# Moving the copies of ten units' transposed q and k from VectorE to ScalarE, with twelve buffers instead of eight for the loads of q and k

## The chip, the core and the metric

The kernel runs on one core of a Trainium2 chip. The engines have short names here: PE is TensorE's matmul and PEld its weight load, DVE is VectorE, ACT is ScalarE, POOL is GpSimd, SP is SyncE. Each engine works through its own list of instructions in order and waits on semaphores for the others. The metric is the device time in microseconds of one execution; the median of three is 149.7 us (148.23 to 149.87).

## The reference

Two stages are chained. The first is attention inside chunks of 64 positions, for 8 batches, 8 heads and 9 chunks each, with a head dimension of 64:

```python
scores = scale * np.matmul(q_c, k_c.transpose(0, 1, 2, 4, 3))     # per chunk, 64 x 64
scores = scores - np.max(scores, axis=-1, keepdims=True)
attn = np.exp(scores)
attn = attn / (np.sum(attn, axis=-1, keepdims=True) + 1e-09)
out = np.matmul(attn, v_c)
```

Its output, put to x of shape (8, 576, 512), goes through a token mixer, batch by batch:

```python
wq = x @ w_q                                   # 512 -> 64
wk = x @ w_k
W_tok = scale * np.einsum('bsd,btd->bst', wq, wk)
mixed = np.einsum('bst,btd->bsd', W_tok, x)
return (np.maximum(mixed, 0.0) @ w_out).astype(np.float32)
```

## The kernel before

The attention is cut into 36 **units** of 16 chunks; four and a half units make a batch. A unit goes through a pipeline of stages, one unit entering in each **period** kk of the main loop:

- `stage_a1` (tile `tp`, L396): 16 transposes of the unit's q and k on PE, eight for q and then eight for k, into one of four PSUM banks of the pool that most other matmuls share.
- `stage_a2` (tile `qkt`, L406): one copy of 128x1024 f16 from that bank into SBUF, on DVE. This is the instruction that the change touches.
- `stage_b1`, `stage_b2`: the scores on PE (`sp`, L422), their maximum (`mx`, L430) and the subtraction (`sh`, L436) on DVE, the exponential on ACT (`es`, L444).
- `stage_c`: transposes of the exponentials on PE (`ep`, L452) and their copy on ACT (`et`, L454).
- `stage_d1`, `stage_d2`: the product with v on PE (`xp`, L468), with a column of ones that gives the denominator, and on DVE the sum, the reciprocal (L480, L482) and the scaling into `x_nat` (L483).

The program is recorded in the order in which it is written, so each engine's list has this order. In period kk that is: scores and maximum of unit kk, product with v of unit kk-2, the mixer's steps of place 0, transposes of unit kk+2, transposes and copy of the exponentials of unit kk-1, subtraction and exponential of unit kk, scaling of unit kk-2, the `qkt` copy of unit kk+2, and the mixer's steps of place 2. The start differs: period 0 also makes stage a of unit 1, and period 1 that of units 2 and 3. So the copy of unit u stands in period u-2 from unit 4 on.

The mixer of a batch begins when its units are done. `make_moe` holds its steps: transposes of x (`tx`, copy `xt` on ACT, L166), products with w_q and w_k (`wpa`, `wpb`, copies `wqkT`), transposes of wk (`wknp`, `wkn`), the product g (L271), the mixed rows (`ma`, relu `rmx`, L172) and the last product with w_out (`op`, L340, copy `osb`, store on SP's queue). `plan` gives each step a period. For batch 0 the first copy of x comes in period 4, the products with w_q and w_k in period 8, `rmx` in periods 11 and 12. After the last period the steps that are left are called in an order written by hand.

Loads of q, k and v change f32 to f16 and go through POOL's queue. Their order is a list sorted by the period of need, and `AHEAD` sets both how many buffers q and k have and how early a load is recorded:

```python
wanted = [(max(u - 2, 0), 1, load_qk, (u,)) for u in range(NU)]
...
        wanted.append((first + 2, 0, load_v, (b, part)))
wanted += [(8, 2, load_wqk, ()), (13, 2, load_wout, ())]
wanted.sort(key=lambda x: x[:2])
```

POOL's list holds hardly anything but these loads, so the recorded place of a load among the stages does not matter to it; what holds a load back is its waits. There are two kinds. A load into a buffer of q or k that was used before waits for the transposes (L396) of the unit that had it. And a load waits for the landing of the load eight places before it, since the loads share eight completion semaphores in turn. v has three buffers for each part. All loads of q and k after unit 0's are at L96, those of v at L106.

Of the kernel before, what the change touches and what calls it, by code (L numbers as in the profile page):

```python
# [17 lines left out]
def kernel(  # L18
# [16 lines left out]
    nc = tc.nc  # L35
# [9 lines left out]
    NU = B * NI // 8  # L45
    W0 = 5 * CH
    R, G = 4, 16
    AHEAD = 8
    scale_attn = 1.0 / math.sqrt(D)
    scale_moe = 1.0 / math.sqrt(DH)  # L50
    ds = bass.ds
# [1 line left out]
    const = ctx.enter_context(tc.tile_pool(name="const", bufs=1))  # L53
    qn_pool = ctx.enter_context(tc.tile_pool(name="qn", bufs=AHEAD))
    v_pool = ctx.enter_context(tc.tile_pool(name="vpool", bufs=3))
# [76 lines left out]
    def loads(before):  # L132
        while wanted and wanted[0][0] < before:
            _, _, load, args = wanted.pop(0)
            load(*args)
# [10 lines left out]
    make_identity(nc, ident[:])  # L146
    loads(AHEAD - 2)

# [16 lines left out]
    def copy(on_vector, to, of):  # L165
        (nc.vector.tensor_copy if on_vector else nc.scalar.copy)(to, of)  # L166
# [222 lines left out]
    def stage_a1(u):  # L389

        tp = bank([P, 2, 8, R, G], F16, name="tp")
        for ti in range(2):
            src = data[u, ti]
            for r in range(R):
                for sl in range(2):
                    nc.tensor.transpose(  # L396
                        tp[CH * sl : CH * sl + CH, ti, :, r, :],
                        src[:, sl, r * D : r * D + D],
                        ident[:],
                    )  # L400
        state[u] = {"tp": tp}

    def stage_a2(u):
        tp = state[u]["tp"]
        qkt = qkt_pool.tile([P, 2, 8, R * G], F16, name="qkt", tag="qkt")
        nc.vector.tensor_copy(  # L406
            qkt[:].rearrange("p t c k -> p (t c k)"),
            tp[:].rearrange("p t c r g -> p (t c r g)"),
        )
        state[u]["qkt"] = qkt  # L410
# [112 lines left out]
    def stage_a(u):  # L523
        stage_a1(u)
        loads(u - 1 + AHEAD)
        stage_a2(u)
# [4 lines left out]
    for kk in range(NU - 1):  # L531
        stage_b1(kk)
        if kk >= 2:
            stage_d1(kk - 2)
        fill(kk, 0, 0.0)
        if 2 <= kk < NU - 2:
            stage_a1(kk + 2)
            loads(kk + 1 + AHEAD)
        if kk >= 1:
            stage_c(kk - 1)  # L540
        stage_b2(kk)
        if kk >= 2:
            stage_d2(kk - 2)
        if 2 <= kk < NU - 2:
            stage_a2(kk + 2)
        for u in ((1,), (2, 3))[kk] if kk < 2 else ():
            stage_a(u)
        fill(kk, 2, 1.4 if len(outs) < 4 else 1.9)
# [17 lines left out]
    u = NU - 1  # L566
# [62 lines left out]
```

## Time and profile before

| | |
|---|---|
| median of 3 runs | 149.7 us (148.23 to 149.87) |
| profiled execution | 149.79 us, its span 148.0 us |
| busy PE / DVE / ACT / POOL | 123.6 / 114.4 / 101.7 / 86.4 us of the span |
| `qkt` copies on DVE (L406) | 36, 24.5 us, mean 680 ns |
| `et` copies on ACT (L454) | 36, 21.5 us, mean 597 ns; ACT idle before them 20.9 us |
| loads of q and k issued by POOL (L96) | 78, 56.1 us busy |

The span is what the trace covers; 1.79 us of the profiled time lie outside it. The page cuts the span into 40 slices of 3.7 us. A row of a group gives the line, engine, operation, tiles and shapes, the count, the busy time, the mean of one, and the idle time of the engine just before it with what ended that. A row of the timeline gives start, duration and the same idle time in brackets. Matmuls overlap, so the gap from one start to the next is what a matmul costs its engine, not its own duration. The same holds more weakly for DVE and ACT, where a duration reaches a little past the start of the next instruction.

### The profile page before, as it was taken

What the parts mean: (1) busy time and instruction counts of PE and PEld (TensorE: products, weight loads), DVE (VectorE), ACT (ScalarE), POOL (GpSimd) and SP (SyncE); (2) the same over time, 40 slices, a digit from 0 to 9 for tenths busy, and PEclk for the clock granted to TensorE, in tenths of its full rate; (3) what the DMA queues carried; (4) which work ended last, traced back from release to release, by engine and by line L of the source; (5) the groups of instructions that cost most, each with busy time, mean ns of one, the idle gap of its engine ahead of it and who ended that gap; (6) DMA issues with size and microseconds to landing.
All of it is one profiled execution on the core that took longest, in us unless ns stands there. A gap on an engine that the chain in (4) does not pass through costs nothing.

```text
span 148.0 us, 5933 instructions
## 1 busy us (share of the span) xinstructions
PE 123.6 (84%) x2516; PEld 82.6 (56%) x2516; DVE 114.4 (77%) x236; ACT 101.7 (69%) x200; POOL 86.4 (58%) x138
## 2 busy tenths in 40 slices
PE   0666999697779899899999999999949998999940
PEld 0454678475666556766576567655635464543420
DVE  0489899999999889989998999899876886156430
ACT  3140356378698699888988998799829995775320
POOL 6999999399996879499269857986000000000000
PEclk9999999779999999999999999999999999999999
DMA  4999999999999999999999999999990623234492
GB/s 141 137 159 161 165 178 166 117 118 149 154 157 185 187 205 228 212 213 207 200 238 187 196 247 220 157 240 200 212 148 21 192 95 126 79 138 142 173 296 104
DMA packets 64619, 25.35 MB, mean 171 GB/s; under 512 B 40528, under 2 KB 60112, under 8 KB 64592
## 3 DMA queue, kind: packets, MB, share of 16 engines
q0 software_dynamic: 58176, 14.56, 103.7%
q1 hardware_dynamic: 6272, 10.28, 20.6%
q8 instruction: 20, 0.33, 0.9%
q10 hardware_dynamic: 144, 0.13, 0.3%
q14 instruction: 7, 0.06, 0.2%
HBM read 29.62 MB, written 9.44 MB: 264 GB/s over the span
## 4 chain that ended last, share of the span: by engine, by line
PE 35%; DVE 29%; ACT 17%; issue 6%; POOL 5%; DMA 3%; DVEq 0%; ACTq 0%; POOLq 0%
PE op L340 13%; DVE x_nat L483 7%; DVE sh L436 7%; DVE mx L430 6%; DVE qkt L406 5%; PE tp L396 5%; ACT es L444 4%; POOL qn L96 4%; PE ep L452 3%; ACT et L454 3%; DMA qn<-in_k_dram 3%; ACT rmx L172 3%; ACT osb L166 3%; PE wknp L244 3%; PE gp L263 2%
## 5 line engine op out<-in xcount | busy, mean ns | idle before, releaser
L454 ACT COPY et<-ep 128x512 f16<-128x512 f16 x36 | 21.5, 597 | 20.9 <-PE ep L452 20.9
L396 PE MATMUL tp<-ident,qn 128*64 128x128 f16 x576 | 27.1, 245 | 8.2 <-DVE qn L144 4.3
L96 POOL DMA_DIRECT2D qn<-in_k_dram x39 | 27.9, 720 | 9.0 <-DMA vt<-in_v_dram 3.1
L96 POOL DMA_DIRECT2D qn<-in_q_dram x39 | 28.2, 727 | 5.3 <-DMA vt<-in_v_dram 1.0
L340 PE MATMUL op<-wout,rmx 128*128 128x512 f16 x124 | 30.5, 379 | 0.7 <-ACT et L454 0.4
L106 POOL DMA_DIRECT2D vt<-in_v_dram x32 | 28.2, 903 | 1.5 <-issue 1.2
L430 DVE TENSOR_REDUCE mx<-sp 128x8 f32<-128x512 f32 x36 | 24.6, 684 | 5.4 <-PE sp L422 5.0
L396 PEld LDWEIGHTS <-qn 128*64 128x64 f16 x576 | 21.6, 124 | 12.2 <-issue 6.2
L436 DVE TENSOR_TENSOR sh<-sp,mx 128x512 f32<-128x512 f32 x36 | 24.9, 692 | 3.6
L406 DVE COPY qkt<-tp 128x1024 f16<-128x1024 f16 x36 | 24.5, 680 | 2.9 <-PE tp L396 2.8
L444 ACT ACTIVATE es<-sh 128x512 f16<-128x512 f32 x36 | 23.3, 647 | 3.7 <-DVE sh L436 3.7
L483 DVE TENSOR_TENSOR x_nat<-xp,rec 128x512 f16<-128x512 f32 x36 | 24.9, 691 | 1.2
L166 ACT COPY osb<-op 128x512 f32<-128x512 f32 (+1 forms) x29 | 17.0, 591 | 7.3 <-PE op L340 5.7
L166 ACT COPY xt<-tx 128x768 f16<-128x768 f16 (+1 forms) x23 | 18.1, 787 | 0.9 <-PE tx L190 0.9
L340 PEld LDWEIGHTS <-rmx 128*128 128x128 f16 x124 | 11.3, 97 | 11.6 <-issue 1.2
L468 PE MATMUL xp<-vt,et 64*64 64x65 f16 x576 | 12.2, 202 | 5.4 <-DVE x_nat L483 2.6
L422 PEld LDWEIGHTS <-qkt 64*64 64x64 f16 x576 | 8.3, 116 | 13.6 <-issue 9.3
L172 ACT ACTIVATE rmx<-ma 128x512 f16<-128x512 f32 x28 | 15.6, 626 | 0.1
L452 PE MATMUL ep<-ident,es 128*128 128x128 f16 x144 | 15.6, 236 | 0.0
L422 PE MATMUL sp<-qkt 64*64 64x64 f16 x576 | 12.3, 208 | 2.8 <-DVE qkt L406 1.9
L468 PEld LDWEIGHTS <-et 64*64 64x64 f16 x576 | 9.3, 113 | 7.1 <-ACT es L444 2.6
L190 PE MATMUL tx<-ident,x_nat 128*128 128x128 f16 x144 | 13.0, 231 | 0.0
(49 smaller groups left out, 142.3 us busy)
## 6 DMA issues: line engine op xcount, KB each, us to landing
out_dram<-osb SPq DMA_DIRECT2D x31, 256.0 KB, 4.1
qn<-in_q_dram POOLq DMA_DIRECT2D x31, 128.0 KB, 6.1
qn<-in_k_dram POOLq DMA_DIRECT2D x31, 128.0 KB, 5.7
vt<-in_v_dram POOLq DMA_DIRECT2D x16, 160.0 KB, 6.3
vt<-in_v_dram POOLq DMA_DIRECT2D x16, 128.0 KB, 7.3
out_dram<-osb SPq DMA_DIRECT2D x9, 128.0 KB, 2.5
qn<-in_q_dram POOLq DMA_DIRECT2D x8, 64.0 KB, 5.6
qn<-in_k_dram POOLq DMA_DIRECT2D x8, 64.0 KB, 5.1
```

The source lines that it names most:

```text
L96: nc.gpsimd.dma_start(tl[p0 : p0 + pn], of[at : at + pn])
L106: nc.gpsimd.dma_start(vt[CH * sl : CH * sl + CH, :, 0:D], of[sl, :, n0:n1, :])
L166: (nc.vector.tensor_copy if on_vector else nc.scalar.copy)(to, of)
L340: nc.tensor.matmul(op[:], lhsT=rmx[:, i, ds(t * P, P)], rhs=wout16[:, i, :], start=(i == 0), stop=(i == HQ - 1),)
L396: nc.tensor.transpose(tp[CH * sl : CH * sl + CH, ti, :, r, :], src[:, sl, r * D : r * D + D], ident[:],)
L406: nc.vector.tensor_copy(qkt[:].rearrange("p t c k -> p (t c k)"), tp[:].rearrange("p t c r g -> p (t c r g)"),)
L430: nc.vector.tensor_reduce(mx[:], sp, axis=AX.X, op=ALU.max)
L436: nc.vector.tensor_tensor(out=sh[:].rearrange("p m l (g r) -> p l m g r", g=G, r=R), in0=sp.rearrange("p l m (r g) -> p l m g r", g=G, r=R ...
L444: nc.scalar.activation(es[:], sh[:], AF.Exp, scale=scale_attn)
L454: nc.scalar.copy(et[:], ep[:])
L468: nc.tensor.matmul(xv[CH * par : CH * par + CH, sl, m, :], lhsT=et[rows, m, CH * par : CH * par + CH], rhs=vt[rows, 0 : D + 1], start=True ...
L483: nc.vector.tensor_tensor(out=x_nat[:, 4 * u : 4 * u + 4, :, :].rearrange("p m l d -> p l m d"), in0=xv[:, :, :, 0:D], in1=rec[:, :, :, No ...
```

## The change

`stage_a2` uses the helper `copy(on_vector, to, of)`, which exists already, so that the `qkt` copies of the units 2 to 9, 11 and 12 are made by ACT; the other 26 stay on DVE. `AHEAD` becomes 12. On ACT's list the copy of unit u stands behind the exponential of unit u-2 and ahead of the mixer's steps of place 2 of that period. The order of POOL's loads is as before; the loads of units 8 to 11 now go into buffers that nobody used before, and those from unit 12 on wait for the transposes of unit u-12 instead of u-8.

```diff
-    AHEAD = 8
+    AHEAD = 12
...
     def stage_a2(u):
         tp = state[u]["tp"]
         qkt = qkt_pool.tile([P, 2, 8, R * G], F16, name="qkt", tag="qkt")
-        nc.vector.tensor_copy(
+
+        copy(
+            not (2 <= u < 10 or u in (11, 12)),
             qkt[:].rearrange("p t c k -> p (t c k)"),
             tp[:].rearrange("p t c r g -> p (t c r g)"),
         )
```

## Prediction

> **What bounds the kernel now.** I read the page's busy table first, then the timelines of DVE, PE, ACT and POOL one by one.
>
> ```profile
> PE 123.6 (84%) x2516; PEld 82.6 (56%) x2516; DVE 114.4 (77%) x236; ACT 101.7 (69%) x200; POOL 86.4 (58%) x138
> DMA  4999999999999999999999999999990623234492
> ```
>
> No engine fills the span, so the bound changes from stage to stage. The DMA engines are busy until slice 30 (110 us). One period in the timeline of DVE:
>
> ```profile
> 27.55 0.68 DVE L406 COPY qkt<-tp 128x1024 f16<-128x1024 f16 x1
> 28.15 0.68 DVE L430 TENSOR_REDUCE mx<-sp 128x8 f32<-128x512 f32 x1
> 28.93 0.69 DVE L436 TENSOR_TENSOR sh<-sp,mx 128x512 f32<-128x512 f32 x1
> ...
> 29.97 0.69 DVE L483 TENSOR_TENSOR x_nat<-xp,rec 128x512 f16<-128x512 f32 x1
> 30.57 0.68 DVE L406 COPY qkt<-tp 128x1024 f16<-128x1024 f16 x1
> ```
>
> There is no idle time in brackets: DVE sets a period of 30.57 - 27.55 = 3.02 us here, of which the copy takes 0.60 (start to start). These are the copies of units 8 and 9. So DVE paces this stretch. But other things stand close behind it, first PE (stretches by time: us, then busy us of PE, PEld, DVE, ACT, POOL, granted clock, DMA share, GB/s):
>
> ```profile
> 21.10:24.51 3.41, 3.41 (x79) 2.78 (x76) 3.24 (x7) 2.43 (x5) 3.41 (x5) 1.00 1.69 183
> 24.51:27.93 3.42, 1.92 (x84) 1.45 (x73) 3.25 (x8) 2.22 (x4) 2.36 (x5) 1.00 1.98 167
> 27.93:31.34 3.41, 3.28 (x78) 2.68 (x71) 3.24 (x8) 1.57 (x3) 2.23 (x4) 0.50 0.68 58
> 38.70:46.70 8.00, 6.29 (x182) 4.62 (x180) 7.58 (x17) 7.71 (x16) 7.19 (x12) 1.00 1.52 159
> 44.99:108.10 63.11, 60.44 (x1383) 40.33 (x1380) 57.23 (x119) 56.04 (x116) 45.06 (x69) 1.00 1.63 208
> ```
>
> PE is full until 24.5 and nearly full from 27.9 to 31.3, where its granted clock is half; it is slow before 24.5 too, as the 16 transposes of a unit show:
>
> ```profile
> 14.44 0.42 PE L396 MATMUL tp<-ident,qn 128*64 128x128 f16 x4 [1.06 <-DMA qn<-in_k_dram]
> 22.09 1.07 PE L396 MATMUL tp<-ident,qn 128*64 128x128 f16 x16
> 25.07 0.64 PE L396 MATMUL tp<-ident,qn 128*64 128x128 f16 x16
> L96 POOL DMA_DIRECT2D qn<-in_k_dram x2: 677/682/686, 8.9 to 9.5; - x2
> DMA to landing us min/median/max: 4.0/4.4/4.8
> ```
>
> (The last two are the two k loads that unit 4 waits for.) From 38.7 on ACT is full as well, and from 45 to 108 PE is (60.44 of 63.11). A second thing stands close: the loads. Counting transposes, the group at 53.71 is unit 17's, since 272 = 17 x 16 came before; its k load is the issue at 46.3, which landed 6.6 us later:
>
> ```profile
> 0.00:53.60 53.60, 14.88 (x272) 11.70 (x273) 0.97 1.49 157
> 53.71 0.64 PE L396 MATMUL tp<-ident,qn 128*64 128x128 f16 x16 [0.15 <-ACT xt L166]
> L96 POOL DMA_DIRECT2D qn<-in_k_dram x1: 705/705/705, 46.3 to 46.3; - x1
> DMA to landing us min/median/max: 6.6/6.6/6.6
> ```
>
> It landed at 52.9, and the k half begins about 0.27 behind the group's start, at 53.98. So the load was just 1.0 us early, and by unit 4's k (the second piece landed at 9.5 + 4.8 = 14.3 and was used at 14.44) the wake-up takes 0.14. Whatever is won before unit 17, no more than 0.9 us of it passes this point while the loads stay where they are. Other units have more room.
>
> **The change, part by part.** *DVE loses ten copies*, 10 x 0.60 = 6.0 us of its list. Each counts only where DVE sets the pace.
>
> ```profile
> 24.27 0.40 PE L422 MATMUL sp<-qkt 64*64 64x64 f16 x16
> 25.12 0.68 DVE L430 TENSOR_REDUCE mx<-sp 128x8 f32<-128x512 f32 x1
> ```
>
> Units 2 to 5: nothing. The k load of unit 4 holds PE until 14.44, and PE is slow and full after it until 24.5.
> Units 6 and 7: up to 1.2 us. PE is idle 1.50 of 3.42 in 24.51 to 27.93. I take 0.4 for the first, since PE delivers that period's scores at 24.67 and DVE takes them at 25.12, and 0.6 for the second: DVE is then 1.0 ahead, PE itself about 0.5, because its product with v waits for a scaling that precedes the second copy.
> Units 8 and 9: PE runs at half clock and is idle 0.13 of 3.41, so it keeps between its 0.5 and, if the clock stays up, DVE's 1.0 + 1.2.
> Units 11 and 12: up to 1.2, with DVE as the pace again.
> By 38.7 the lead is thus between 0.5 and 3.4 us. Unit 10 stays on DVE and gives nothing.
>
> *ACT gains ten copies.* No row shows this copy on ACT. The nearest are
>
> ```profile
> L166 ACT COPY xt<-tx 128x768 f16<-128x768 f16 x22 | 17.6, 801 | 0.9 <-PE tx L190 0.9
> L166 ACT COPY xt<-tx 128x384 f16<-128x384 f16 x1 | 0.5, 485 | 0.0
> 30.25 0.63 ACT L444 ACTIVATE es<-sh 128x512 f16<-128x512 f32 x1
> 30.78 0.79 ACT L166 COPY xt<-tx 128x768 f16<-128x768 f16 x1
> 32.29 0.59 ACT L454 COPY et<-ep 128x512 f16<-128x512 f16 x1 [0.72 <-PE ep L452]
> 39.72 0.79 ACT L166 COPY xt<-tx 128x768 f16<-128x768 f16 x1
> 40.57 1.08 ACT L172 ACTIVATE rmx<-ma 128x512 f16<-128x512 f32 x2
> 37.88 0.37 ACT L271 CAST g<-gp 128x256 f16<-128x256 f32 x1 [1.18 <-PE gp L263]
> 32.03 0.30 PE L208 MATMUL wpa<-xt,wqk 128*128 128x320 f16 x1
> ```
>
> 384 more elements cost 801 - 485 = 316 ns, so 1024 elements cost 801 + 211 = 1012 ns; from start to start a tenth less, as es shows (0.63 against 0.53): 0.93 us by estimate, bounds 0.68 (as on DVE) and 1.01. Ten make 9.3 us. Behind each copy on ACT's list stand that period's mixer copies, then `et`, for which PE's product with v waits. Through unit 8 the idle time covers them (ACT is busy 1.53 to 2.43 us of 3.41 in the rows above). Two are not covered. Unit 9's stands ahead of the xt copy at 30.78, whose result the products with w_q use at 32.03, 0.46 behind its end at 31.57: 0.93 - 0.46 = 0.5 at most is exposed. Unit 12's stands ahead of the xt copy at 39.72, in the stretch where ACT is busy 7.71 of 8.00: 0.93 less the idle 0.29, so 0.64 at least, 0.93 at most, is taken off the lead. Unit 11's falls into the idle 1.18 us before g and costs nothing.
> So the lead at 46.7 lies between 0.5 - 0.5 - 0.93 = -0.9 and 3.4 - 0.64 = 2.8; the middle is 1.0, and I take 1.0, since the two ends need the clock to fall and to hold in the same stretch.
>
> The Trainium skill's page "ScalarE: Activation LUTs", section "Rules for kernel authors", speaks against this: it gives simple elementwise work to VectorE, up to about three times faster per element in 16 bits. Three times 0.68 would be 2.04 us a copy, and unit 12's alone would take 1.1 us more from the lead, which leaves no change. The rows above give a ratio of 1.5, so I go by them.
>
> *Twelve buffers.* Unit 17's load at 46.3 took the buffer of unit 9, whose transposes ended before its copy at 30.57. The buffer had been free for 15 us. Eight buffers never held a load back by themselves, so four more give nothing there. What could come is a side effect in POOL's waits:
>
> ```profile
> 27.65 0.71 POOL L96 DMA_DIRECT2D qn<-in_q_dram  x1 [1.02 <-DMA vt<-in_v_dram]
> 29.54 0.72 POOL L96 DMA_DIRECT2D qn<-in_k_dram  x1 [1.18 <-PE tp L396]
> ```
>
> These are unit 11's q and k, behind the weights in the list. The 1.18 us is put down to the buffer's wait on PE, which falls away for units 8 to 11. As unit 3's transposes had long been over, the wait instruction at most costs something: 0 to 1.18 us by which the later loads come earlier, and with them the ceiling of 0.9 rises to 2.1 at most. Unit 34's k landed at 96.3 + 6.8 = 103.1 (rows below), 17 units and 50.2 us after unit 17's: 2.95 us a unit, so the loads are hardly quicker than DVE's 3.02, and what they do not gain here they do not gain later.
>
> *Sum.* Lead 1.0 at 46.7, ceiling 0.9 to 2.1 at unit 17. I take 1.0. From there PE, ACT and DVE are all nearly full, and the shift goes through to the end one to one. 149.79 - 1.0 = **148.8 us**, that is 0.9 under the median of 149.7. Bounds of this case: 149.4 (0.4 left) to 147.9 (the ceiling raised, 1.9).
>
> **The rivals.** *The wait on code goes.* At 108 us PE stops in the middle of unit 34's transposes (one group of 16 comes after it):
>
> ```profile
> 107.70 0.39 PE L396 MATMUL tp<-ident,qn 128*64 128x128 f16 x8
> 110.13 0.41 PE L396 MATMUL tp<-ident,qn 128*64 128x128 f16 x8 [2.04 <-issue]
> L96 POOL DMA_DIRECT2D qn<-in_k_dram x1: 737/737/737, 96.3 to 96.3; - x1
> DMA to landing us min/median/max: 6.5/6.7/6.8
> q8 instruction: 1, 0.02, 2.7%
> PE tp L396 <- issue: 2.0, 1, 2.0
> ```
>
> The load that it needs had landed 5 us before, and in the window of this stop the view of DMA queues shows one packet of instructions. So I read it as PE out of code, because the fetch stood behind the loads. The view of waits (last row: in total, times, longest) has this once, so it hangs on small shifts. Without it: 1.5 us less, which is also the distance of the run of 148.23 from the other two, so 147.3. For it: one of the three times may already be without it. Against: the loads are as dense at that place as before. The Trainium skill's page "Runtime: NRT & Kernel Launch", section "Instruction fetch mechanics", calls the cost of crossing into new code mostly hidden; by that the 2.04 would be no fetch, would come again, and the time would stay at 148.8.
>
> *The lead is lost.* PE's half clock and ACT's full stretch eat it all, the lead at 46.7 is 0: 149.8.
>
> *ACT becomes the bound, slower.* If there is no lead when ACT reaches its full stretch at 38.7, because PE at half clock gave nothing back, then unit 9's and unit 12's copies stand bare in ACT's list, 2 x 0.93 = 1.9 us, and PE's products with v wait behind them: 149.8 + 1.9 = 151.7. For it: the full row 38.70:46.70. Against: 1.50 us of PE's time were idle just before, and DVE paced both sides. It decides when the lead at 38.7 is under 0.9.
>
> *The change doesn't do what it says*, in its second half: I count the twelve buffers at nothing, as above; this is part of the forecast.
>
> **How the numbers follow.** A measurement of this kernel can tell about 1% (1.5 us) from no change; the three times shown differ by that much. Forecast 0.32, and of it 0.08 is below 148.2. Code wait gone 0.25, all faster. Lead lost 0.20, of it 0.06 also without the code wait (149.8 - 1.5, some shift) and so faster. ACT as the bound 0.23, of it 0.22 over 151.2. Faster 0.08 + 0.25 + 0.06 = 0.39; slower 0.22; within 1% the rest, 0.39. The range goes from 146.9 (the code wait gone and a lead of 1.4) to 151.5, which leaves out half of the slow case and the fastest tail. The likeliest case's own range is 147.9 to 149.4.
>
> **What would show it.** In the new profile: `qkt` x10 on ACT at 0.95 to 1.05 us; DVE's period near 2.4 us between 24 and 42 where units 6 to 9, 11 and 12 were moved; unit 17's transposes within 0.3 us of their k landing; POOL's rows after 30 us earlier by at most 1.2; the idle 2 us of PE near 107 there or not. I am wrong if loads are issued much earlier than before, which would mean that buffers did hold them; if PE is still behind at 40 us; or if ACT shows no idle time before `et` from 30 to 47 and DVE waits for it.

## The result, and the profile after

The changed kernel takes 147.95 us in the median of 22 executions (146.46 to 151.99), the kernel before 149.71 us (147.97 to 151.87). The ratio is 0.9869, with a 95% interval of 0.9841 to 0.9897: 1.3% faster; the medians are 1.8 us apart. The ratio leaves out the executions over 1.5% slower than the fastest of their kernel, 9 of the changed kernel and 7 of the other, and the means of the rest are 1.97 us apart. The means of all 22 are 148.66 and 149.89 us, only 1.23 us apart with a standard error of 0.45. The forecast was 148.8 us, 0.6% faster; it had the direction, and the time lies within its range, but it gave half the gain. The profiled execution of the changed kernel took 147.85 us, its span is 146.1 us.

From the page after come the busy times, the granted clock and the share of the DMA engines in 40 slices, and from the view of groups, kept apart by form, the copies of `qkt`:

```profile
PE 122.7 (84%) x2516; PEld 81.1 (56%) x2516; DVE 108.8 (74%) x226; ACT 110.4 (76%) x210; POOL 86.7 (59%) x138
PEclk9999999999999699999999999999999999999996
DMA  4999999999999999999999999999942623135483
L166 DVE COPY qkt<-tp 128x1024 f16<-128x1024 f16 x26 | 17.7, 682 | 1.4 <-PE tp L396 1.4
L166 ACT COPY qkt<-tp 128x1024 f16<-128x1024 f16 x10 | 10.0, 1012 | 0.0
```

The ten copies moved as written: DVE is 5.6 us less busy and ACT 8.7 us more. One copy takes 1012 ns on ACT, which is the estimate of its duration to the nanosecond. DVE's timeline shows what it brings while it lasts, the maxima of units 7 and 8:

```profile
26.09 0.68 DVE L432 TENSOR_REDUCE mx<-sp 128x8 f32<-128x512 f32 x1
28.52 0.68 DVE L432 TENSOR_REDUCE mx<-sp 128x8 f32<-128x512 f32 x1
```

The period is 2.43 us where it was 3.02. By unit 11 the maximum comes 2.9 us sooner than before (37.36 against 40.25 us in DVE's timeline). Then all of it is lost. A first part, 1.15 us, goes by unit 13 (44.56 against 46.30 us). Here ACT has next to no idle time (its timeline from 37.3 to 44.9 us, with unit 12's copy at 37.83), and the transposes of PE wait for that copy, the maximum for its scores:

```profile
38.88 0.96 PE L396 MATMUL tp<-ident,qn 128*64 128x128 f16 x16 [0.85 <-ACT qkt L166]
44.56 0.69 DVE L432 TENSOR_REDUCE mx<-sp 128x8 f32<-128x512 f32 x1 [0.56 <-PE sp L424]
```

The rest goes behind it. The next rows are the first product with w_out in PE's timeline, and two stretches of 3.4 us (us, busy us of PE, its granted clock, DMA share, GB/s), the second of which begins where the clock falls:

```profile
48.08 1.69 PE L340 MATMUL op<-wout,rmx 128*128 128x512 f16 x4 [1.36 <-DMA wout<-in_moe_w_out_dram]
44.86:48.27 3.41, 1.98 (x37) 1.00 1.53 185
48.27:51.69 3.42, 3.42 (x54) 0.50 1.72 191
```

In the kernel before the same product came at 48.43 us; its wait of 0.43 us is put down to ACT, but the weights had landed only 0.14 us before it. Now PE arrives early, waits 1.36 us for the weights, which landed only 0.35 us sooner (47.94 against 48.29 us), and is busy for only 1.98 of 3.41 us. In the stretch that follows it gets half its clock, and what was won is spent. The maxima of units 17 and 35, first of the kernel before and then of the changed one:

```profile
59.33 0.68 DVE L430 TENSOR_REDUCE mx<-sp 128x8 f32<-128x512 f32 x1
118.43 0.68 DVE L430 TENSOR_REDUCE mx<-sp 128x8 f32<-128x512 f32 x1
```

```profile
60.03 0.68 DVE L432 TENSOR_REDUCE mx<-sp 128x8 f32<-128x512 f32 x1
117.09 0.68 DVE L432 TENSOR_REDUCE mx<-sp 128x8 f32<-128x512 f32 x1
```

At unit 17 the changed kernel is 0.70 us behind, at unit 35 it is 1.34 us ahead. So the whole gain of this execution arises in between (57.06 us instead of 59.10, which is 2.04 less), and one row of PE's timeline shows where. It is unit 34's transposes, which stopped for 2.04 us before:

```profile
108.42 0.77 PE L396 MATMUL tp<-ident,qn 128*64 128x128 f16 x16
```

Now the 16 run without a stop. Read from these two traces alone, the copies brought nothing, and the whole gain is a stop that the change has nothing to do with. The experiments show that neither execution stands for its kernel.

### The profile page after: what moved, and what is told of

Its sections match the earlier page's. It is cut to its first block, busy times and chain, and to the rows that moved or that the text cites. A ratio compares the mean times of both kernels' runs of the same rounds, so it can differ in the third digit from the quotient of the medians.

```text
span 146.1 us, 5938 instructions
## 1 busy us (share of the span) xinstructions
PE 122.7 (84%) x2516; PEld 81.1 (56%) x2516; DVE 108.8 (74%) x226; ACT 110.4 (76%) x210; POOL 86.7 (59%) x138
## 4 chain that ended last, share of the span: by engine, by line
PE 43%; DVE 21%; ACT 17%; DMA 7%; issue 5%; POOL 3%; SPq 0%; DVEq 0%; ACTq 0%
PE op L340 13%; PE tp L396 7%; DVE sh L438 6%; DVE mx L432 6%; DMA wout<-in_moe_w_out_dram 5%; DVE x_nat L485 5%; PE ep L454 4%; ACT es L446 4%; ACT et L456 3%; DVE qkt L166 3%; PE sp L424 3%; PE gp L263 3%; ACT osb L166 3%; PE opt L357 2%; PE tx L190 2%
## 5 line engine op out<-in xcount | busy, mean ns | idle before, releaser
L340 PE MATMUL op<-wout,rmx 128*128 128x512 f16 x124 | 31.2, 385 | 1.6 <-DMA wout<-in_moe_w_out_dram 1.4
L396 PE MATMUL tp<-ident,qn 128*64 128x128 f16 x576 | 26.5, 240 | 6.2 <-DVE qn L144 4.3
L166 DVE COPY qkt<-tp 128x1024 f16<-128x1024 f16 x26 | 17.7, 682 | 1.4 <-PE tp L396 1.4
L470 PE MATMUL xp<-vt,et 64*64 64x65 f16 x576 | 11.7, 199 | 5.2 <-DVE x_nat L485 3.1
L454 PE MATMUL ep<-ident,es 128*128 128x128 f16 x144 | 15.1, 231 | 0.1
L470 PEld LDWEIGHTS <-et 64*64 64x64 f16 x576 | 8.8, 112 | 6.9 <-ACT et L456 4.9
L190 PE MATMUL tx<-ident,x_nat 128*128 128x128 f16 x144 | 12.3, 223 | 0.1
```

The lines of the kernel that those rows point to most:

```text
L340: nc.tensor.matmul(op[:], lhsT=rmx[:, i, ds(t * P, P)], rhs=wout16[:, i, :], start=(i == 0), stop=(i == HQ - 1),)
L396: nc.tensor.transpose(tp[CH * sl : CH * sl + CH, ti, :, r, :], src[:, sl, r * D : r * D + D], ident[:],)
L454: nc.tensor.transpose(ep[:, m, :], es[:, m, :, :], ident[:])
```

## The experiments

The measure used below is the start of the maximum of unit 17 and of unit 35: whatever a change in the first 46 us achieves must show at unit 17, and what happens behind it shows in the distance of the two. Each comparison was made on one chip. The kernel before had medians of 149.5 to 151.6 us in them, so ratios are to the kernel before of the same comparison.

### Taking the change apart

Theory A: the lead ends at the loads and w_out near 48 us, and the gain is that PE's stop near 108 us no longer comes. Theory B: the lead of the copies goes through to the end. Theory C: the twelve buffers bring the gain. The first two kernels make one half of the change each, the other two repeat the kernels before and after with one profiled execution.

Copies alone, against the kernel after:

```diff
-    AHEAD = 12
+    AHEAD = 8
```

> The ten copies on ScalarE, with eight buffers as before. Theory A (the lead won by the copies ends at the wait for w_out near 48 us, and the gain is PE's stop of 2 us near 108 us that no longer comes): about 148.0 us, the wait of PE for w_out 1 to 1.5 us long, and no stop of PE over 1 us between 100 and 112. Theory B (the lead of the copies goes through to the end): 148.0 us as well, but then unit 17's and unit 32's maxima earlier than before by 1 us or more (before: 59.32 and 107.13). Theory C (the four more buffers bring the gain): 149.7 us.

Buffers alone, against the kernel before:

```diff
-    AHEAD = 8
+    AHEAD = 12
```

> Twelve buffers, all copies on VectorE as before. Theory A: the buffers do not hold any load, so the loads land as before within 0.5 us and the time is 149.7 us with the stop near 108 us, or 148.2 without it. Theory B: 149.7. Theory C: 148.0 us, with unit 11's loads and all later ones issued 1 us earlier.

The kernel before again:

> The kernel before once more, for its profile. Theory A: PE stops again for 1.5 to 2.5 us near 108 us with no data missing, and the execution takes 149.2 to 149.9 us; if the stop is missing, 147.9 to 148.4. Theory B: the stop comes and goes without a matching difference in time.

The kernel after again:

> The changed kernel once more, for its profile. Theory A: PE waits 1 to 1.5 us for w_out at 47 us, the maxima of units 17 to 32 are within 1 us of the kernel before, no stop of PE over 1 us between 100 and 112; 146.5 to 148.2 us. Theory B: the maxima of units 17 to 32 are 1 us or more earlier than before.

| | median us | ratio to before (151.56) | unit 17, us | unit 35, us |
|---|---|---|---|---|
| copies alone | 149.37 (147.15 to 151.69) | 0.977, 0.971 to 0.984 | 59.27 | 120.69 |
| buffers alone | 149.22 (148.74 to 151.55) | 0.986, 0.980 to 0.991 | 58.76 | 119.38 |
| before again | 152.27, one execution | | 59.94 | 121.06 |
| after again | 149.14, one execution | | 58.56 | 118.09 |

Each half alone gained as much as both together, which no theory had expected, though the scatter leaves the sizes loose. The wait for w_out was 0.78 and 0.79 us with the copies, less than theory A had it, and the clock did not fall. The changed kernel's second profile is 0.77 us ahead at unit 17 (59.33 in the first profile of the kernel before), where its first was 0.70 behind. And the stop at 108 us alone is not the matter. In the waits of PE and its timeline, stops for which nothing else is to blame stand at other places, or with the buffers alone at this one; here the longest of the kernel before again, of the copies alone, and of the buffers alone:

```profile
76.51 0.38 PE L452 MATMUL ep<-ident,es 128*128 128x128 f16 x4 [2.68 <-issue]
```

```profile
75.43 0.25 PE L396 MATMUL tp<-ident,qn 128*64 128x128 f16 x2 [1.59 <-issue]
```

```profile
109.93 0.45 PE L396 MATMUL tp<-ident,qn 128*64 128x128 f16 x8 [1.86 <-issue]
```

The kernel before stopped for 2.04 us at 108 in one execution and for 2.68 at 73.8 and 0.81 at 82.9 in another. So whether a stop comes, and how long it is, differs between executions of one kernel, and theory A in its first form, this one stop, falls.

### What the stop is

From here theory A says: the gain is fewer or shorter such stops, wherever they fall. Four kernels ask what makes them. The first leaves out the last load of v, with zeros in its place:

```diff
-        for sl in range(2):
+        if b == B - 1 and part == 1:
+            nc.gpsimd.memset(vt[:, :, 0:D], 0.0)
+        for sl in range(2) if (b, part) != (B - 1, 1) else ():
             nc.gpsimd.dma_start(vt[CH * sl : CH * sl + CH, :, 0:D], of[sl, :, n0:n1, :])
```

> The kernel before, without the last load of v (batch 7, inputs 16 to 35; zeros stand in their place): the loads end some 2.5 us sooner, all else is as it was. Theory A (now: the changed kernel gains only by shorter stops of PE for its program code, and such a stop comes where PE enters a new block of code while the load packets are dense): PE enters a block near 103.8 us with few packets in flight, the stop of 2.0 us near 108 is gone, 0.985 to 0.99 of the time of before; stops at other places (67 to 90 us) come as often as before. Theory B (the lead of ScalarE's copies): no lead is made here, ratio 1.00, the stop stays. Theory C (the twelve buffers bring loads forward): the loads' end is what counts, so it agrees with A on the sign, 0.985 to 0.99.

It took 149.9 us (147.06 to 153.74), the ratio is 0.979 (0.971 to 0.986). The stop was still there, at 108.4 us, with 1.21 us instead of 2.04: a miss for theory A's detail. The time scatters too much to say more.

The second moves PE's code by 128 instructions, with 64 small matmuls (each with its weight load) while PE has nothing to do yet:

```diff
+    z = const.tile([P, 16], F16, name="z")
+    nc.vector.memset(z[:], 0.0)
+    zp = x_psum.tile([P, 2, 512], F32, name="zp", tag="xp")
+    for j in range(64):
+        nc.tensor.matmul(zp[0:16, 0, 0:16], lhsT=z[:], rhs=z[:], start=True, stop=True)
     stage_a(0)
```

> The kernel before with 64 small matmuls on zeros ahead of the first transposes, while PE waits for the first loads: all later code of PE stands 128 instructions further on, half a block, and every block begins some 3 us sooner in the work. Theory A: the stops of PE come 193 instructions behind multiples of 256 of the new count, so the one at 108.1 us goes to about 105 or vanishes; the time moves by up to 2 us to either side, 0.985 to 1.00. Rival: the stop is no matter of code but of what PE does at that place (a wait that the trace does not show): it stays at the same work, 108.1 us, ratio 1.00. Theory B and C: 1.00.

149.59 us, 0.989 (0.981 to 0.996). The stretches from the start to inside the stop (us, then busy us and instructions of PE, PEld, DVE, ACT, POOL, clock, DMA share, GB/s), for the kernel before and for this one, and the stop's end in this one:

```profile
0.00:109.90 109.90, 92.95 (x2130) 65.92 (x2130) 94.99 (x194) 79.39 (x155) 86.44 (x138) 0.98 1.55 185
```

```profile
0.00:106.70 106.70, 89.80 (x2130) 64.07 (x2130) 91.40 (x189) 77.00 (x150) 86.83 (x138) 0.95 1.58 185
106.91 0.40 PE L452 MATMUL ep<-ident,es 128*128 128x128 f16 x4 [0.66 <-ACT wkn L166]
```

Both stops stand behind 2130 matmuls and 2130 weight loads, 64 of each being the added ones in the second. In the work the stop has moved: it stood in the middle of unit 34's transposes and now comes earlier, behind a whole group of 16. So the place is one in the code and not in the work. (The profile blames a copy on ACT for the 0.66; it is named because its semaphore came last.) The two stops of the kernel before again fit this too: 1364 + 1365 and 1492 + 1492 instructions lie ahead of them in the trace, 255 apart, and from there to 4260 it is 1276, five times 255. PE's code thus comes in blocks of about 255 recorded instructions, and a stop can only come at one place of each block. The traces also show what PE waits for. The page has the packets of the instruction queue in each execution, 16 KB each:

```profile
q8 instruction: 20, 0.33, 0.9%
```

In the kernel before one of them began at 107.82 us and ended at 108.82, and the stop ended 1.31 us later, at 110.13. In all twenty traces there are 34 stops of at least 0.15 us for which nothing else is to blame. For 33 of them a packet of this queue ends 1.27 to 1.61 us before PE goes on, and 173 to 181 recorded instructions over a multiple of 255 lie ahead of them; the one left over is 0.16 us long. The stop of 0.66 us above ends 1.50 us behind such a packet, so it is one of them too. In every execution the packets take 1.0 to 1.2 us on average, with few stops or many, so what makes a stop is a packet that began late.

The third kernel leaves out the stores of batches 0 to 4, 24 of 41 stores; their matmuls and evictions stay:

```diff
-                nc.sync.dma_start(out[b, ds(t * P, P), :], osb[:])
+                if b >= B - 3:
+                    nc.sync.dma_start(out[b, ds(t * P, P), :], osb[:])
...
-            for o in range(2):
+            for o in range(2) if b >= B - 3 else ():
```

> The kernel before without the stores of batches 0 to 4 (their matmuls and evictions stay): this leaves the software queue's loads (1.3 to 1.7 of the DMA time from 68 to 108 us) and takes the stores' 0.19 to 0.25 away until about 110 us. If the store packets delay PE's code, the stops go and the time is 0.975 to 0.985. If the loads of the software queue delay it, as theory A has it after the traces, the stops stay: 0.99 to 1.00. Theory B and C: 1.00.

147.08 us, 0.974 (0.969 to 0.980), and its six executions lie between 146.27 and 147.97 us, where those of the kernel before go from 149.88 to 151.92. No stop of 0.15 us or more is left. I had held the loads for the cause, because they take most of the DMA engines' time; but taking away the stores is enough to end the stops. The stretch from 90 to 110 us, of the kernel before and of this one (columns as above):

```profile
90.00:110.00 20.00, 17.59 (x409) 11.61 (x406) 17.76 (x37) 16.44 (x34) 11.18 (x17) 1.00 1.57 206
```

```profile
90.00:110.00 20.00, 19.51 (x434) 12.98 (x431) 18.13 (x38) 17.72 (x37) 6.23 (x10) 1.00 0.97 89
```

Without the stores the loads also end sooner (POOL has 10 instructions left here instead of 17). Whether the store packets delay the packets of PE's code themselves or by stretching the loads was not told apart.

The fourth asks for the other half, the lead. It is the kernel after with the output products held until period 15, so that none waits for w_out:

```diff
-        while outs and outs[0][0] == place and spent + outs[0][1] <= budget:
+        while kk >= 15 and outs and outs[0][0] == place and spent + outs[0][1] <= budget:
```

> The kernel after, with the first output matmuls held back until period 15, so that nothing waits for w_out at 46.6 to 48.0 us. If w_out's landing alone ends the lead (A, first reading): the maximum of unit 14 starts 1.5 to 2.5 us sooner than in the kernel after (50.2), that of unit 17 at 58.0 to 59.0 instead of 60.0, and the clock does not fall at 48. If the q and k loads end it (A, second reading): unit 14 is sooner by 1 us, unit 17 at 59 to 60 all the same. Time in both readings within 0.5 % of the kernel after (0.985 to 0.99 of before), as the output matmuls held back are made up later on a full PE. Theory B (lead goes through): 0.975 to 0.98.

148.15 us (147.51 to 150.63), 0.980 (0.974 to 0.986). Unit 14 comes at 48.74 us instead of 50.18, unit 17 at 58.90 instead of 60.03, and the clock does not fall. From unit 13 to unit 17 it takes 13.2 us (45.70 to 58.90) where the profiled execution of the kernel after took 15.5 (44.56 to 60.03), so there the wait for w_out and the half clock behind it cost 2.3 us. Behind unit 17 this execution has four stops of 2.8 us in sum, so nothing can be said on the end from it.

### Without the stops

With the stops gone the lead can be seen by itself. The stores are left out as above in the kernels after and before:

> The kernel after without the stores of batches 0 to 4. Theory A (the change gains only because PE stops less for its code, and nothing of the lead reaches the end): with the stops gone in both, this kernel stands within 0.5 % of the kernel before without the same stores (147.1 us, 0.974 of before): 146.4 to 147.8. Theory B (the lead goes through and the stops are another matter): it is faster than that kernel by what the change brought, 1.3 %: 145.2, 0.961.

> The kernel before without the stores of batches 0 to 4 once more, for the comparison on the same chip: 0.97 to 0.98 of before in every theory, no stop of PE over 0.3 us for its code.

Then the full work, with those 24 stores held in 22 more buffers and issued from period 31 on, three per period, the rest in the drain; both for the kernel after and for the kernel before:

```diff
-    osb_pool = ctx.enter_context(tc.tile_pool(name="osb", bufs=8))
+    osb_pool = ctx.enter_context(tc.tile_pool(name="osb", bufs=30))
...
-                nc.sync.dma_start(out[b, ds(t * P, P), :], osb[:])
+                save(out[b, ds(t * P, P), :], osb[:], b < B - 3)
...
         fill(kk, 2, 1.4 if len(outs) < 4 else 1.9)
+        if kk >= 31:
+            flush(3)
```

> The kernel after, with the stores of batches 0 to 4 held in 22 more buffers and issued from period 31 on, three per period, when the loads are nearly done, the rest between the steps of the drain. If the stores among the loads are what delays PE's code (A): stops gone until 104 us; 146.5 to 147.5, 0.975 of before, unless the stores crowd the drain. Rival: the 24 stores (5.8 MB) come on top of the drain's 3.8 MB, and the last store waits for them: 149 to 152, 0.99 to 1.01. Theory B: 145.5 to 146.5.

> The kernel before with the stores held in the same way. A: within 0.5 % of the kernel after with late stores (146.5 to 147.5 if the drain bears them). B: slower than that kernel by 1.3 %. Rival of the crowded drain: 149 to 152 here as there.

| | median us | ratio to before (150.40) |
|---|---|---|
| after, few stores | 145.93 (145.05 to 147.28) | 0.974, 0.968 to 0.979 |
| before, few stores | 147.29 (146.33 to 147.73) | 0.983, 0.978 to 0.988 |
| after, late stores | 145.89 (145.56 to 147.95) | 0.974, 0.969 to 0.978 |
| before, late stores | 147.12 (146.17 to 147.50) | 0.982, 0.977 to 0.987 |

The stops are gone but for one of 0.3 us in each execution with late stores. Both pairs have the same sign: by the medians the changed kernel is 1.4 and 1.2 us faster, by the means 1.1 and 0.6, each with an error of 0.4. So theory A's claim that nothing arrives hardly holds, and theory B's 1.3% is too much. But the profiled executions do not show it. With few stores the changed kernel is even 0.84 us behind at unit 17 (60.12 against 59.28). The rows are the maxima of units 17 and 35, of the kernel before and then of the kernel after, both with late stores:

```profile
60.26 0.68 DVE L441 TENSOR_REDUCE mx<-sp 128x8 f32<-128x512 f32 x1
117.15 0.68 DVE L441 TENSOR_REDUCE mx<-sp 128x8 f32<-128x512 f32 x1
```

```profile
60.32 0.68 DVE L443 TENSOR_REDUCE mx<-sp 128x8 f32<-128x512 f32 x1
117.21 0.68 DVE L443 TENSOR_REDUCE mx<-sp 128x8 f32<-128x512 f32 x1
48.54 1.87 PE L351 MATMUL op<-wout,rmx 128*128 128x512 f16 x4 [1.49 <-DMA wout<-in_moe_w_out_dram]
44.80:48.20 3.40, 2.01 (x64) 1.00 1.38 185
48.20:51.60 3.40, 3.06 (x44) 0.50 1.84 185
```

From unit 17 to unit 35 it is 56.89 us in both, to the last digit. The changed kernel has no lead at unit 17, and its rows show the same wait for w_out and the same fall of the clock as in the first profile. This execution took 147.37 us, the second longest of its seven. So four more kernels were run, to see an execution without that fall and to tell the halves apart: late stores with the copies alone, with the buffers alone, with the outputs held besides, and as before.

> Late stores with ScalarE's copies alone (eight buffers). If the copies make the lead and the buffers add nothing, as the prediction had it: the time of the whole change with late stores (145.9 us, 0.970 to 0.974 of before). If the buffers make it: 147.1, 0.982, as the kernel before with late stores.

> Late stores with the twelve buffers alone (all copies on VectorE). If the copies make the lead: 147.1 us, 0.982, as the kernel before with late stores. If the buffers bring it: 145.9, 0.972.

> The whole change with late stores and with the output matmuls held until period 15, so that no wait for w_out stops PE at 46.6 to 48.4 us and its clock does not fall for 3.4 us behind that. If that fall is what ate the lead in the profiled executions: unit 17's maximum at 58.5 to 59.5 instead of 60.3, the time 145.0 to 145.9 and closer together than without the hold (145.6 to 147.9). If the lead is lost to the q and k loads whatever w_out does: unit 17 at 60, 145.9 to 147.

> The whole change with late stores once more, for the comparison on the same chip: 145.5 to 148, median 145.9, 0.970 to 0.974 of before; in executions without the clock's fall at 48 us, unit 17 about 1 us sooner than 60.3.

| | median us | ratio to before (149.52) | unit 17, us | unit 35, us |
|---|---|---|---|---|
| copies, late stores | 146.32 (145.44 to 147.51) | 0.980, 0.975 to 0.985 | 58.90 | 115.80 |
| buffers, late stores | 145.86 (145.50 to 147.42) | 0.978, 0.973 to 0.983 | 59.35 | 116.24 |
| both, outputs held | 147.16 (145.99 to 147.65) | 0.984, 0.979 to 0.989 | 59.19 | 116.66 |
| both | 145.92 (145.35 to 146.40) | 0.977, 0.973 to 0.981 | 57.90 | 114.78 |

The last kernel is the one whose profile showed no lead a moment ago. Its rows now, in the same order:

```profile
57.90 0.68 DVE L443 TENSOR_REDUCE mx<-sp 128x8 f32<-128x512 f32 x1
114.78 0.68 DVE L443 TENSOR_REDUCE mx<-sp 128x8 f32<-128x512 f32 x1
47.48 1.02 PE L351 MATMUL op<-wout,rmx 128*128 128x512 f16 x4 [0.48 <-ACT et L467]
44.80:48.20 3.40, 2.68 (x63) 1.00 1.71 183
48.20:51.60 3.40, 3.40 (x91) 1.00 1.67 195
```

The weights landed 1.06 us sooner here (47.34 instead of 48.40 us), PE was busy for 2.68 of the 3.40 us, the clock held, and unit 17 comes 2.4 us sooner than in the other execution of the same kernel. All of it arrives at unit 35: 114.78 - 57.90 = 56.88. So what an execution is ahead at unit 17 goes through. In the ten profiles with few or late stores and no outputs held, the whole time is unit 17's start plus 87.0 to 87.5 us, so the kernels differ there by what happens before unit 17.

What sets unit 17 can be read from all twenty traces together. Where PE comes before the weights, the first product with w_out starts 0.13 to 0.14 us behind their landing. In nine of these executions, five with the copies on ACT and four with them on DVE, the maximum of unit 17 follows that start by 10.41 or 10.42 us; in the first profile of the kernel before it is 10.90, and in the two whose clock falls near 48 us 11.78 and 11.95. And the weights do not land sooner with the copies: at 47.3 to 49.6 us with them, at 47.3 to 50.0 without. By these traces a lead over w_out is lost, and the copies help only where PE would come late. Without them it came 0.2 to 1.9 us behind the landing in six of eleven executions; with them, and the outputs not held, in none of seven. This goes with the clock: a stretch of half clock begins between 26 and 42 us in ten of the eleven executions without the copies, and in one of the nine with them.

The mean start of unit 17 is 59.30 us in the seven and 59.67 in the eleven, 0.4 us apart with an error as large. The traces alone thus do not confirm the size of the gain.

Holding the outputs did keep the clock up, but the products held back are made up for on a full PE: behind unit 17 it took 0.6 us longer, and the kernel is 1.2 us slower than without the hold.

The buffers alone were as fast as both. Since the kernel before with late stores stood in another comparison, the two were run side by side:

> The kernel before with late stores, once more. If the buffers alone gain about 1 us, this kernel is at 147.1 us again, 1 us over the one with twelve buffers; if the two comparisons only differed, both are within 0.4 us of each other, at 146 to 147.

> Late stores with the twelve buffers alone, once more: 145.9 us and 1 us under the kernel before with late stores if the buffers gain; within 0.4 us of it if they do not, as the prediction had it.

147.03 us (146.22 to 148.17) against 146.51 us (145.89 to 147.52), ratios 0.983 (0.974 to 0.992) and 0.978 (0.970 to 0.985): the intervals overlap, so this pair is inconclusive. Taking all executions with late stores together, the means are 147.07 us for the kernel before (12), 146.32 for the buffers (12), 146.36 for the copies (6) and 146.17 for both (13), each with a standard error of 0.2 to 0.3. Buffers alone are thus faster by 0.75 us with an error of 0.3 (0.20 and 0.19 added as squares), across chips. The traces show no way in which they could. POOL's timeline has the loads of unit 11's k and unit 17's k, of the kernel before and then of the buffers alone, both with late stores:

```profile
29.30 0.72 POOL L96 DMA_DIRECT2D qn<-in_k_dram  x1 [1.32 <-PE xp L479]
45.87 0.72 POOL L96 DMA_DIRECT2D qn<-in_k_dram  x1
```

```profile
29.75 0.72 POOL L96 DMA_DIRECT2D qn<-in_k_dram  x1 [1.10 <-DVE rec L493]
46.20 0.71 POOL L96 DMA_DIRECT2D qn<-in_k_dram  x1
```

The wait of 1.18 us that the prediction had put down to the buffer is there with twelve buffers too, and the loads are not issued sooner. So what the buffers do stays open. It also leaves open which half of the change makes its gain: beside the buffers alone, the copies add 146.32 - 146.17 = 0.15 us, less than the error.

The whole change with late stores is also, level with the buffers alone with late stores, the fastest full kernel here: 0.974 and 0.977 of the kernel before in its two comparisons, 145.9 us both times.

## Where the prediction was right and where it was wrong

- **ACT's copy at 1012 ns**: measured 1012. From start to start it is 0.89 and 0.92 us for units 12 and 11, where 0.93 was taken. The Trainium skill's page "ScalarE: Activation LUTs", section "Rules for kernel authors", would have it up to three times slower than VectorE; the ratio of the two rows is 1012 / 682 = 1.5.
- **Units 2 to 5 gain nothing**: missed in the profiled execution, by luck of the clock. Unit 6's maximum came at 23.66 instead of 25.12 us, already 1.5 ahead, with PE's clock full from 21.0 us on instead of 24.5. When the clock changes differs between executions of the same kernel: the kernel before again had it at half until 22.8 us. The clock column prints 1.00 up to the first record of the clock, so the row 21.10:24.51 of the prediction does not show a full clock; unit 7's transposes take 1.07 us there and 0.64 in the kernel after.
- **Lead by 38.7 between 0.5 and 3.4**: 2.9 at unit 11. **By 46.7 between -0.9 and 2.8, taken 1.0**: 1.7 at unit 13 (44.56 against 46.30). The part taken off for ACT's full stretch, 0.64 to 0.93 us, measured 1.15. That the clock holds in the kernel after and not in the kernel before was one of the two ends named; in the kernel before it fell at 27.9 us.
- **Ceiling of 0.9 at unit 17's k load, "other units have more room"**: the wrong load. In the profiled execution that k landed at 52.4 us and was used at 54.6, so it held nothing. What ends a lead is w_out, which the sum does not have: its second piece landed at 48.29 us, 0.14 us ahead of its use in the kernel before. I had not looked at it, since in the profile before the wait of the product that needs it is put down to ACT. In the profiled execution of the kernel after, the 1.7 us of unit 13 were -0.70 at unit 17.
- **What is ahead at unit 17 goes through one to one**: right, where the stops are gone. With few or late stores the distance from unit 17 to unit 35 is 56.88 to 56.90 us in every profile, except the one with the outputs held. With the stores in place it is 57.06 to 61.42.
- **A gain of 1.0 from this lead**: the size fits, 1.2 to 1.4 by the medians without stops, 0.9 by the means with late stores (147.07 - 146.17). But that it is the lead of the copies is not shown, since the buffers alone gain 0.75. A size that comes out on a path that was wrong at w_out is in part luck.
- **The stop for code**: this is the step that failed. The sum started from an execution with a stop of 2.04 us and kept it on both sides, and a rival with a chance of 0.25 had it gone. In the two profiled executions it is the whole gain: -0.70 at unit 17 and 2.04 behind it make the 1.34 at unit 35. The runs show the stops as a varying cost of every kernel with its stores in place, 0.5, 2.7, 3.9 and 5.6 us in sum in four profiles with the copies on ACT, and 1.4 to 3.6 in five without. By these the changed kernel does not stop less. By the medians the stops (and whatever else those stores cost) come to 149.71 - 147.1 = 2.6 us before and 147.95 - 145.9 = 2.0 us after; this is a difference between separate comparisons, in which the kernel before alone goes from 149.5 to 151.6, so the 0.6 between them shows nothing. How the gain comes to be twice the forecast thus stays open in part: about 1 us is there without the stops as well, and the rest may be stops or scatter. The Trainium skill's page "Runtime: NRT & Kernel Launch", section "Instruction fetch mechanics", calls the cost of a new block mostly hidden. At most blocks the traces agree, at a few they show up to 2.68 us.
- **ACT as the bound, slower**: did not come as a slower kernel. The ten copies had no idle time before them (0.0 in their row), but PE's waits put down to a `qkt` of ACT's come to 0.8 us before transposes and 0.7 before scores. What ACT's full stretch took is the 1.15 us of lead named above.
- **Twelve buffers give nothing**: right for the loads, by POOL's rows above, and unsettled for the time.

## What to carry to other kernels

A lead made early in a kernel is worth what the next late load lets through, so look at every load on the way and not only at the one that waits now; a load 0.14 us early is a wall for any lead. One profiled execution is one draw, so read the landing and the wake-up in several before naming the wall. Before a single stop is put into a sum as fixed, see whether it comes in a second execution at the same place. When a gain and the scatter are of one size, take the source of the scatter away in both kernels (here by moving stores) and compare again.

## What the runs showed of the hardware

- PE's program code arrives in blocks of about 255 recorded instructions (20 packets of 16 KB for 5032 of them), and PE can stop once per block at a fixed place, for 0.2 to 2.7 us, until 1.3 to 1.6 us after the end of a packet that began late. The sum of such stops in a profiled execution went from 0.5 us (kernel after) to 5.6 (copies alone), and none of 0.15 us or more came where the stores were left out. Moving 5.8 MB of stores out of the loads' way made the kernel before 1.8% faster (0.982, 0.977 to 0.987), against the 1.3% of the change.
- PE's clock is granted in stretches of 3.41 us. In these traces it falls from full to half only behind a stretch in which PE was busy for at most 2.26 us (1.98 and 2.01 in the rows above), and held at 2.68 of 3.40. A low share does not always bring the fall: the clock held behind 1.66 us in the kernel before (106.43 to 109.84 us), and behind 2.01 us in the kernel before with late stores, once more (47.34 to 50.75 us, with a wait of 1.40 us for w_out). The Trainium skill's page "TensorE: Matmul & The Clock Gate", section "HAM oscillation — how this bites in real kernels", warns of idle gaps of more than about 3.4 us; here the clock fell behind a single wait of 1.36 us.
